# A gated SSM-convolution and token-mixing kernel on one Trainium2 core: more sums by accumulating transfers, small vector work on ScalarE, another fixed order

## The chip, the cores and the metric

The kernel runs on one core of a Trainium2 chip (trn2). The metric is the device time of one execution in microseconds (us); the kernel before took 177.37 us, the median of three runs (177.35 to 178.18). Profiles are of one execution each. The engines are called as the profile calls them: PE (TensorE, with its weight loads as PEld), DVE (VectorE), ACT (ScalarE), POOL (GpSimd) and SP (SyncE, which here only issues transfers).

## What is computed

Two branches over S = 2048 tokens and D = 640 channels are mixed by a gate:

```python
x = A_q                                              # (1, 2048, 640) bf16, like k and v
g = sigmoid((x * gate_w).sum(-1, keepdims=True))
# branch a: k is shifted by a 4-tap causal filter, multiplied with v, then convolved over the
# tokens with a kernel of length 2048 per channel (reference: FFTs of length 4096)
kv = k_shift * v
a  = q * (irfft(rfft(kv) * rfft(ssm_k)) + kv * ssm_D)
# branch b: layer norm of x over channels, then an MLP over the tokens (2048 -> 1536 -> 2048)
h = layernorm(x)
u = gelu(einsum("bsd,sf->bdf", h, w1) + b1)
b = (einsum("bdf,fs->bds", u, w2) + b2).transpose
out = g * a + (1 - g) * b
```

## The kernel before

**Tiling.** A token row tile is 128 tokens by 640 channels; there are 16, in four groups hk of four (p = 0 to 3), all in SBUF in `X`. The matrix `ssm` (640 channels by 2048 taps) is loaded in five blocks of 128 channels, which I number 0 to 4. The transforms are matrix products with cosine and sine tables: `FE` is made on the chip, `FO` is loaded (two transfers of 256 KB), `GTB` holds the inverse tables.

**Stages on PE.** (1) A few matmuls on zeros (`spin`), then per ssm block two transpositions (`transp`, eight 128x128 matmuls for each half h of the taps) and four table products (`wblock`, 16 matmuls each); ACT or DVE copies every result out of PSUM: `wT` after a transposition, `Wb` after a table product. For h = 0, POOL first adds `ssm_D` to column 0 of the block, and that value comes from a tiny matmul and the ACT copy `dcol`. (2) The first MLP product (`m1`: 12 tiles of F, four groups of eight 128x320 matmuls each; ACT applies gelu and writes `GT`), mixed with the shift filter (`kv`, which needs the DMA transposes of k in `KT`) and the forward transforms (`A`). (3) The second MLP product (`m2`, 16 tiles of 24 matmuls; ACT writes `O1` with scale `omg` and bias `c2`). (4) The inverse transforms (`inv`), for h = 0 and h = 1 and four values of p; ACT scales each by the gate (`cg`), DVE multiplies by q and the sum with `O1` leaves by a transfer of 320 KB.

**DVE** does the layer-norm statistics (`ln_tile`: two bn_stats of 320 columns and a bn_aggr per tile), part of the normalization (`ln_apply`), the sums and differences of the transforms (`mixing`, `invmix`, `halved`), the complex products (`product`, `cross`) and the end of the last tile (`last_stt`). A tensor_tensor works on 2560 or 5120 columns there. Some sums are not done on DVE but by a transfer that POOL issues and that adds into its destination (`accum=True`): `v1mix`, `mixing_acc`, `acc_dma`, the second half of some products (the `late` branch), and the output of h = 0.

**What sets the order.** Everything is first recorded as operations with numbers, then emitted in the order of the string `_ORDER` (line 1318 on); each engine runs its own instructions in that order and waits by semaphores for what it depends on. `_ENG` says for 50 operations (copies from PSUM, normalizations, permutations of k) whether ACT or DVE does them, `_SLOTS` which of four PSUM buffers each group of matmuls takes; the group must wait until that buffer's last contents are copied out. So one late operation holds back everything behind it on its engine. SP issues the loads in the same order, and the loads of the start all go through one queue.

**Lines in the profile.** L298 is every matmul, L556 every tensor_tensor, L600 ACT's `act`, L615 and L616 the copies of `either` on ACT and DVE, L627 `last_stt`, L267 an accumulating transfer, L272 a plain one, L265 a DMA transpose, L897 and L899 the statistics, L914 and L915 the normalization on ACT and DVE.

**The last tile.** Row tile (hk 3, p 2) is multiplied last, as two times twelve matmuls: one half of the 640 columns, then the other (`last_`), each 320 wide. `last_stt` combines each half with scale and gate part, and one transfer writes the 160 KB.

Of the kernel before, what the change touches and what calls it, by code (L numbers as in the profile page):

```python
# [9 lines left out]
BF16 = mybir.dt.bfloat16  # L10
# [422 lines left out]
def _build(nc, A_q, A_k, A_v, A_shift_k, A_ssm_k, A_ssm_D, B_x, B_w1, B_b1, B_w2, B_b2, gate_w, out):  # L433
# [10 lines left out]
    with ExitStack() as es:  # L444
# [27 lines left out]
        def base_of(h):  # L472
            return T.mem[h.name][1]
# [24 lines left out]
        cst = alloc("cst", [128, 2], F32)  # L498
# [27 lines left out]
        ksh = [alloc(f"ksh{i}", [128, 4, D], BF16, at=base_of(GT) + 5120 * (1 + i)) for i in range(2)]  # L526
        rows = alloc("rows", [20, 5, 512], BF16, at=base_of(GT))
# [139 lines left out]
        def dr(t, off, ap):  # L667
            return bass.AP(tensor=t.tensor, offset=t.offset + off, ap=ap)
# [23 lines left out]

        def x_load(hk):
            dma(X[:, hk, :, :], qrow(hk), 128 * 5120, chain=True, rate=(352.0 if hk == 0 else 415.0))
# [28 lines left out]
        ssm_load(0, 0, 1)  # L723
        for a, b in ((0, 1), (1, 4)):
            dma(X[:, 0, a:b, :], dr(A_q, a * D, [[4 * D, 128], [1, (b - a) * D]]), 128 * 1280 * (b - a), chain=True)
        ssm_load(1, 0, 1)
        for db in range(1, ND):
            dma(ssm[:, db, :], dr(A_ssm_k, 128 * S * db, [[S, 128], [1, S]]), 128 * 4096, chain=True)
        for p in range(2):
            dma(FO[:, p, :, :, :, :].rearrange("q a b c d -> q (a b c d)"), dr(odd_tab, 1024 * p, [[2048, 128], [1, 1024]]), 128 * 2048, chain=True)  # L730
        for hk in range(1, 4):
            x_load(hk)
# [14 lines left out]
        memset("DVE", cst[:, 1:2], -0.5)  # L747
        iota = lambda ap, pat, b, cm: nolock("POOL", 0.1 + n_of(ap) / 1100.0, lambda s: T.op("POOL", lambda e: e.iota(ap, pat, base=b, channel_multiplier=cm), [], [ap]), [], [ap])
# [152 lines left out]

        def ln_scale(a, b):
            n = b - a
            ts("POOL", sd[:, a:b], mv[:, a:b, 1], 1e-5, None, ALU.add, prio=0)
            o_ = tt("POOL", rstd[:, a:b], sd[:, a:b], V(cst, 1, [[0, n]]), ALU.pow, prio=0)
            o_.dur, o_.lock = 1.75, False
            tt("POOL", sd[:, a:b], sd[:, a:b], rstd[:, a:b], ALU.mult, prio=SDP)
            tt("POOL", nb[:, a:b], mv[:, a:b, 0], rstd[:, a:b], ALU.mult)
            ts("POOL", nb[:, a:b], nb[:, a:b], -1.0, None, ALU.mult)
# [17 lines left out]
        for h in range(2):  # L927
# [5 lines left out]
            if h == 0:  # L933
# [20 lines left out]
                def stats_of(k):  # L954
                    for t in range(LB[k], LB[k + 1]):
                        b0, b1, ag = ln_tile(t // 4, t % 4)
                        b0.after.update(seq[-1:])
                        seq.append(b0)
                        flush()
                        b1.after.update(seq[-1:])  # L960
                        seq.append(b1)
                        pag.append(ag)
                    ln_scale(LB[k], LB[k + 1])
# [12 lines left out]
                mixing(C[0], SS, 0, fine=True, prio=MIXP)  # L976
# [104 lines left out]
        ts("DVE", gpre[:, :], mv[:, :, 0], gws[:, 0:1], None, ALU.mult, mode=1)  # L1081
        tt("DVE", gpre[:, :], gpre[:, :], gth[:, :], ALU.add, mode=1, prio=0)
        act(gth[:, :], gpre[:, :], ACT.Tanh, scale=0.5, prio=0)
        ts("DVE", gg[:, :], gth[:, :], 0.5, 0.5, ALU.mult, ALU.add, mode=1, prio=0)
        ts("DVE", omg[:, :], gth[:, :], -0.5, 0.5, ALU.mult, ALU.add, mode=1, prio=0)
# [20 lines left out]

        INVP = ((0, 2, 1, 3), (1, 3, 0, 2))
        for hk, p in [(hk, p) for hk in range(2) for p in range(4)] + [(hk, p) for p in INVP[1] for hk in (2, 3)]:
# [7 lines left out]
            for a in range(na):  # L1116
                items = []
                for ft, ci in order[a * (24 // na):(a + 1) * (24 // na)]:
                    items.append((chk(ci), w2t(hk, p, ft), GT[:, ft, 320 * ci:320 * ci + 320], ft == 0, ft == FT - 1))
                mms(vt, items, name="m2")  # L1120
                if last_:
                    vt.keep = True
                    lastvt.append(vt)
# [22 lines left out]
        def product(dst, a, v, late=None, into=None):  # L1146
# [14 lines left out]
            tt("DVE", P2(T1), P2(a), P2(v, True), ALU.mult)  # L1161
            tt("DVE", H(dst, 0), H(T0, 0), H(T0, 1), ALU.subtract)
            tt("DVE", H(dst, 1), H(T1, 0), H(T1, 1), ALU.add)
# [32 lines left out]
        def invmix(Ya, Yb, sc, bfirst=False, behind=None):  # L1196
# [8 lines left out]
            for (hy, sy), k in (((hb, sb), 1), ((ha, sa), 0)) if bfirst else (((ha, sa), 0), ((hb, sb), 1)):  # L1205
                tt("DVE", sl(hs, ss + k), sl(hy, sy), sl(hy, sy + 1), ALU.add)
                tt("DVE", sl(hy, sy), sl(hy, sy), sl(hy, sy + 1), ALU.subtract)
# [27 lines left out]
        def inverse(h, Z, G=None):  # L1235
            for p in INVP[h]:
# [24 lines left out]
                tt("DVE", qv if h == 0 else cg[:, :, :], cg[:, :, :], qv, ALU.mult)  # L1261
                if h == 1 and p == INVP[1][-1]:
# [4 lines left out]
                    for ci in range(2):  # L1267
                        last_stt(O1[:, 3, p, 320 * ci:320 * ci + 320], chk(ci), omg[:, t:t + 1], cg[:, 1, 320 * ci:320 * ci + 320], lastvt[ci])
                    dma(rows_of(1, p, 1, 1), O1[:, 3, p, :], 128 * 1280, sem="out")
                elif h == 0:  # L1270
                    dma(ov, qv, 128 * 2560, stream="POOL", prio=0, accum=True)
                    dma(rows_of(0, p, 0, 2), ov, 256 * 1280, sem="out")
# [19 lines left out]
        chained(product, A1[1], A1[1], V0[1], tmp_of(q_hi, 0), V1[1])  # L1292
        chained(product, A1[0], A1[0], V0[0], tmp_of(q_hi, 1), V1[0])
        acc_dma(A1[1], V1[1])
        acc_dma(A1[0], V1[0])
        chained(product, A0[1], A0[1], V0[1], H(V0[1], 0))
        lastacc = SC.ops[-1]
        assert lastacc.eng == "POOL"
        for kt in range(2):
            dma(q_hi[:, kt, :, :], qrow(kt), 128 * 5120, wait=[H(A0[1], 1)]).deps.add(lastacc)  # L1300
        chained(product, A0[0], A0[0], V0[0])
        for kt in range(2):
            dma(q_lo[:, kt, :, :], qrow(2 + kt), 128 * 5120)
# [37 lines left out]
"""  # L1341
_ENG = "DAAAAADDAAAAAADDDDDAAADDDADDDDADDAAAAAAAAAAAAAAADD"
_SLOTS = "1120021323201331122022011133001030332021001010110220110131230121002123231321103301332230032032101133201012203121332133113300113"
# [26 lines left out]
```

## Time and profile before

| | |
|---|---|
| median of the runs (lowest to highest) | 177.37 us (177.35 to 178.18) |
| the profiled execution | 177.12 us |
| its span in the profile | 175.1 us |
| PE / PEld busy | 170.0 / 138.2 us |
| DVE / ACT / POOL busy | 168.9 / 107.6 / 42.7 us |
| granted PE clock | full in all 40 slices |
| moved by transfers | 44.06 MB, mean 252 GB/s |
| accumulating transfers, 640 KB | 15: 8 C<-C, 4 C<-q_hi, 3 C<-SS; median 8.8, 9.7 and 7.4 us from issue to landing |
| accumulating transfers into O, 320 KB | 4; median 4.3 us |

The profiled execution took 2.0 us more than its span; that part lies around the span. Times below are from the span's start. "Busy" counts the instructions' own times: matmuls are pipelined, so a busy PE may still be held up between two of them, and the distance between the starts of two groups is the better measure of PE's pace.

### The profile page before, as it was taken

Reading aid. Unit: us, or ns where it says so; the run is one execution under the profiler, and the core shown is the slowest. Engines: PE = TensorE matmul, PEld = TensorE weight load, DVE = VectorE, ACT = ScalarE, POOL = GpSimd, SP = SyncE. Lnnn points to the kernel's source line nnn. Section 1 sums busy time; section 2 is a strip of 40 time slices with the busy share of each in tenths; the row PEclk is TensorE's granted clock in tenths of the full one; section 3 lists DMA queues with packets and bytes.
Section 4 is the critical chain, followed back from the end, with each engine's and each line's share of the span. In section 5 each row is a group of like instructions: output and inputs, shape, how many; then the busy total and the mean of one; then the engine's idle time right before and its main releaser. Section 6 shows DMA issues by size and latency. Waiting matters only on the chain.

```text
span 175.1 us, 3683 instructions
## 1 busy us (share of the span) xinstructions
PE 170.0 (97%) x1559; PEld 138.2 (79%) x1559; DVE 168.9 (96%) x187; ACT 107.6 (61%) x160; POOL 42.7 (24%) x62
## 2 busy tenths in 40 slices
PE   7999999999899999999999999999999999999992
PEld 2599999877697767777777778888899998698782
DVE  7899999999999999999999999999999999999984
ACT  4499999997999997877556214222215105645760
POOL 3199891000000650003202202220055000052200
PEclk9999999999999999999999999999999999999999
DMA  5999999999999799992999999999939999549598
GB/s 144 397 421 405 376 200 225 380 375 221 179 383 356 172 192 192 186 358 57 178 174 365 353 211 349 282 207 240 300 108 187 197 177 372 241 65 209 106 233 292
DMA packets 33248, 44.06 MB, mean 252 GB/s; under 512 B 12112, under 2 KB 24656, under 8 KB 33104
## 3 DMA queue, kind: packets, MB, share of 16 engines
q1 hardware_dynamic: 28024, 32.68, 57.6%
q0 software_dynamic: 5168, 11.14, 37.4%
q8 instruction: 12, 0.20, 0.4%
q14 instruction: 4, 0.03, 0.1%
q10 hardware_dynamic: 40, 0.01, 0.0%
HBM read 27.44 MB, written 2.62 MB: 172 GB/s over the span
## 4 chain that ended last, share of the span: by engine, by line
PE 93%; DMA 3%; ACT 2%; DVE 0%; DVEq 0%; SPq 0%; issue 0%
PE pp L298 93%; DMA ssm<-in_A_ssm_k_dram 3%; ACT L600 1%; ACT ksh L600 1%; ACT GT L600 0%; DVE O L627 0%; DVEq L426 0%; SPq L272 0%
## 5 line engine op out<-in xcount | busy, mean ns | idle before, releaser
L298 PE MATMUL pp<-X,ring 128*128 128x320 bf16 x384 | 55.4, 299 | 0.5 <-ACT GT L600 0.5
L556 DVE TENSOR_TENSOR C<-C 128x2560 bf16<-128x2560 bf16 (+2 forms) x38 | 54.6, 1485 | 0.3 <-ACT C L600 0.2
L298 PE MATMUL pp<-GT,W 128*128 128x320 bf16 x384 | 53.6, 299 | 0.0
L298 PEld LDWEIGHTS pp<-GT,W 128*128 128x128 bf16 x384 | 48.0, 129 | 4.6
L298 PEld LDWEIGHTS pp<-X,ring 128*128 128x128 bf16 x384 | 37.0, 98 | 15.0 <-ACT GT L600 0.8
L600 ACT ACTIVATE O<-pp,c,omg 128x640 bf16<-128x640 f32 x15 | 12.9, 883 | 24.8 <-PE pp L298 24.8
L267 POOL DMA_DIRECT2D C<-C x8 | 10.5, 1674 | 51.1 <-DVE C L556 30.0
L600 ACT ACTIVATE C<-pp 128x640 bf16<-128x640 f32 x32 | 20.4, 711 | 2.0 <-PE pp L298 2.0
L600 ACT ACTIVATE cgb<-pp,gg 128x640 bf16<-128x640 f32 x16 | 12.1, 795 | 13.3 <-PE pp L298 7.6
L615 ACT ACTIVATE C<-pp 128x1024 bf16<-128x1024 f32 x18 | 17.1, 1051 | 0.3 <-PE pp L298 0.3
L600 ACT ACTIVATE gq<-gq 128x640 bf16<-128x640 bf16 x16 | 11.6, 727 | 5.7 <-DVE gq L556 5.7
L556 DVE TENSOR_TENSOR tm<-C,C 128x5120 bf16<-128x5120 bf16 x5 | 14.1, 2819 | 0.1
L897 DVE BATCH_NORM_STATS2 stats<-X 128x6 f32<-128x320 bf16 x32 | 13.1, 470 | 0.4 <-DMA X<-in_A_q_dram 0.2
L298 PE MATMUL pp<-wT,FO 128*128 128x128 bf16 x160 | 12.4, 219 | 0.0
L600 ACT ACTIVATE GT<-pp,cc 128x640 bf16<-128x640 f32 x12 | 9.3, 793 | 4.8 <-PE pp L298 4.7
L298 PE MATMUL pp<-C,GTB 128*128 128x320 bf16 x80 | 11.9, 299 | 0.0
L298 PE MATMUL pp<-wT,FE 128*128 128x128 bf16 x120 | 11.7, 219 | 0.0
L556 DVE TENSOR_TENSOR SS<-C 128x2560 bf16<-128x2560 bf16 x8 | 11.7, 1482 | 0.0
L267 POOL DMA_DIRECT2D O<-q_hi x4 | 4.8, 1324 | 27.7 <-DVE q_hi L556 27.7
L600 ACT ACTIVATE ksh<-pp 128x1024 bf16<-128x1024 f32 (+1 forms) x12 | 10.1, 908 | 1.4 <-PE pp L298 1.3
L267 POOL DMA_DIRECT2D C<-q_hi x4 | 4.8, 1198 | 23.8 <-DVE q_hi L556 10.9
L556 DVE TENSOR_TENSOR C<-tm 128x2560 bf16<-128x2560 bf16 x7 | 10.3, 1487 | 0.1
(92 smaller groups left out, 225.3 us busy)
## 6 DMA issues: line engine op xcount, KB each, us to landing
ring<-in_B_w_dram SPq DMA_DIRECT2D x12, 512.0 KB, 8.8
W<-in_B_w_dram SPq DMA_DIRECT2D x12, 512.0 KB, 6.8
C<-C POOLq DMA_DIRECT2D x8, 640.0 KB, 8.8
kn<-in_A_k_dram SPq DMA_DIRECT2D x4, 640.0 KB, 9.6
C<-q_hi POOLq DMA_DIRECT2D x4, 640.0 KB, 9.7
out_dram<-O SPq DMA_DIRECT2D x7, 320.0 KB, 3.2
ssm<-in_A_ssm_k_dram SPq DMA_DIRECT2D x4, 512.0 KB, 7.0
X<-in_A_q_dram SPq DMA_DIRECT2D x3, 640.0 KB, 7.3
```

The lines of the kernel that those rows point to most:

```text
L267: ins = engobj.dma_start(out_ap, in_ap, accum_op=ALU.add, max_dma_last_dim=2560)
L298: ins = self.nc.tensor.matmul(ps_ap, lhsT=lhsT, rhs=rhs, start=start, stop=stop, skip_group_check=True)
L556: o_ = SC.add(eng, d, lambda s: T.op(eng, lambda e: e.tensor_tensor(o, a, b, op), rd, [o]), rd, [o], prio=prio, name="tt")
L600: return T.op("ACT", lambda e: e.activation(o, src, func, **kw), rr + [src], ww)
L615: return either(name, o, i, [], lambda e, src: e.activation(o, src, ACT.Copy, **kw), lambda e, src: e.tensor_copy(o, src) if scale == 1.0 ...
L897: ops.append(SC.add("DVE", 0.38, (lambda o, i: lambda s: T.op("DVE", lambda e: e.bn_stats(o, i), [i], [o]))(o, i), [i], [o]))
```

## The change

- **Loads.** X group 1 in place of group 0 is loaded in two pieces, ssm block 4 in place of block 0 in two halves (`xpart`, `ssm_load`).
- **Row tile 11** (hk 2, p 3) has its mean and variance made on ACT (`ln_tile_act`, three instructions) instead of on DVE (three).
- **Gate.** `gpre`, `gg` and `omg` are scaled on ACT instead of DVE; a constant 0.5 is set by POOL.
- **Mixing** of `C[0]`: one sum and one difference of 5120 columns instead of two of 2560 each; the same in `invmix` for the second half.
- **Products.** All four now take the branch with an accumulating transfer; A0[0] took the one without. A0 comes first, then A1 with its sum by transfer; the q loads follow.
- **Output of h = 1.** For p = 1 and 3 the sum with `O1` is an accumulating transfer and then the output transfer, in place of a DVE sum.
- **Last tile.** 512 and 128 columns in place of 320 and 320, and two output transfers.
- **Order.** New `_ORDER`, `_ENG` and `_SLOTS`. In the new order the operation `table`, a tiny gelu that makes ACT load that function's table, stands right behind the sine that makes `FE`; in the old one it stood behind the first gelu results. SP's first loads are: before X group 2, ssm block 1, half of block 0, block 2, the two FO, X group 3, block 3, X group 1, 480 KB of X group 0; after X group 2, ssm block 0, half of block 4, X group 0, block 3, 160 KB of X group 1, the two FO, 480 KB of X group 1, block 1, X group 3, block 2.

```diff
-        ssm_load(0, 0, 1)
+        ssm_load(0, 4, 5)
         for a, b in ((0, 1), (1, 4)):
-            dma(X[:, 0, a:b, :], dr(A_q, a * D, [[4 * D, 128], [1, (b - a) * D]]), 128 * 1280 * (b - a), chain=True)
-        ssm_load(1, 0, 1)
-        for db in range(1, ND):
+            dma(X[:, 1, a:b, :], xpart(1, a, b), 128 * 1280 * (b - a), chain=True)
+        ssm_load(1, 4, 5)
+        for db in [d for d in range(ND) if d != 4]:
...
+        def ln_tile_act(t):
+            xs = X[:, t // 4, t % 4, :]
+            r = 1.0 / math.sqrt(D)
+            act(junk[:, :], xs, ACT.Copy, scale=1.0 / D, acc=mv[:, t, 0:1], name="lnm")
+            act(cst[:, 2:3], mv[:, t, 0:1], ACT.Copy, scale=-r, name="lnb")
+            act(junk[:, :], xs, ACT.Square, scale=r, bias=cst[:, 2:3], acc=mv[:, t, 1:2], name="lnm")
...
-                mixing(C[0], SS, 0, fine=True, prio=MIXP)
+                mixing(C[0], SS, 0, prio=MIXP)
...
-        ts("DVE", gpre[:, :], mv[:, :, 0], gws[:, 0:1], None, ALU.mult, mode=1)
+        act(gpre[:, :], mv[:, :, 0], ACT.Copy, scale=gws[:, 0:1])
         tt("DVE", gpre[:, :], gpre[:, :], gth[:, :], ALU.add, mode=1, prio=0)
         act(gth[:, :], gpre[:, :], ACT.Tanh, scale=0.5, prio=0)
-        ts("DVE", gg[:, :], gth[:, :], 0.5, 0.5, ALU.mult, ALU.add, mode=1, prio=0)
-        ts("DVE", omg[:, :], gth[:, :], -0.5, 0.5, ALU.mult, ALU.add, mode=1, prio=0)
+        act(omg[:, :], gth[:, :], ACT.Identity, scale=-0.5, bias=cst[:, NCST:NCST + 1], prio=0)
+        act(gg[:, :], gth[:, :], ACT.Identity, scale=0.5, bias=cst[:, NCST:NCST + 1], prio=0)
...
+        LASTC = (0, 512, 640)
...
+                    c0, c1 = LASTC[ci:ci + 2] if last_ else (320 * ci, 320 * ci + 320)
...
+            if ha is hb and sb + 2 == sa:
+                y0, y1 = (V(ha, (sb + j) * SL, [[2 * SL, 2], [1, SL]]) for j in range(2))
+                tt("DVE", V(hs, (ss + 1) * SL, [[-SL, 2], [1, SL]]), y0, y1, ALU.add)
+                tt("DVE", y0, y0, y1, ALU.subtract)
...
-                tt("DVE", qv if h == 0 else cg[:, :, :], cg[:, :, :], qv, ALU.mult)
+                by_dma = h == 0 or p in (1, 3)
+                tt("DVE", qv if by_dma else cg[:, :, :], cg[:, :, :], qv, ALU.mult)
...
-                        last_stt(O1[:, 3, p, 320 * ci:320 * ci + 320], chk(ci), omg[:, t:t + 1], cg[:, 1, 320 * ci:320 * ci + 320], lastvt[ci])
-                    dma(rows_of(1, p, 1, 1), O1[:, 3, p, :], 128 * 1280, sem="out")
-                elif h == 0:
+                        c0, c1 = LASTC[ci:ci + 2]
+                        last_stt(O1[:, 3, p, c0:c1], (lambda s, ci=ci, n=c1 - c0: s[:, 512 * ci:512 * ci + n]), omg[:, t:t + 1], cg[:, 1, c0:c1], lastvt[ci])
+                        o_ = rows_of(1, p, 1, 1)
+                        dma(bass.AP(tensor=o_.tensor, offset=o_.offset + c0, ap=[list(o_.ap[0]), [1, c1 - c0]]), O1[:, 3, p, c0:c1], 128 * 2 * (c1 - c0), sem="out")
+                elif by_dma:
                     dma(ov, qv, 128 * 2560, stream="POOL", prio=0, accum=True)
-                    dma(rows_of(0, p, 0, 2), ov, 256 * 1280, sem="out")
+                    dma(rows_of(h, p, 0, 2), ov, 256 * 1280, sem="out")
...
-        chained(product, A1[1], A1[1], V0[1], tmp_of(q_hi, 0), V1[1])
-        chained(product, A1[0], A1[0], V0[0], tmp_of(q_hi, 1), V1[0])
-        acc_dma(A1[1], V1[1])
-        acc_dma(A1[0], V1[0])
-        chained(product, A0[1], A0[1], V0[1], H(V0[1], 0))
...
-        chained(product, A0[0], A0[0], V0[0])
...
+        for g in range(2):
+            chained(product, A0[g], A0[g], V0[g], tmp_of(tm[1], g))
+        for g in (1, 0):
+            chained(product, A1[g], A1[g], V0[g], tmp_of(q_hi, g), V1[g])
+            acc_dma(A1[g], V1[g])
```

More of the change, by code (lines that the diff above doesn't have):

```diff
@@ L497, in _build @@
         c2 = alloc("c2", [128, 16], F32)
-        cst = alloc("cst", [128, 2], F32)
+        NCST = 3
+        cst = alloc("cst", [128, NCST + 1], F32)
         FE = alloc("FE", [128, 2, 2, 2, 128], BF16)
@@ L526, in _build @@
         ksh = [alloc(f"ksh{i}", [128, 4, D], BF16, at=base_of(GT) + 5120 * (1 + i)) for i in range(2)]
+        junk = alloc("junk", [128, D], BF16, at=base_of(GT) + 10240)
         rows = alloc("rows", [20, 5, 512], BF16, at=base_of(GT))
@@ L691, in qrow, with xpart @@
             return row8(A_q, hk) if hk >= 2 else dr(A_q, 512 * hk * D, [[4 * D, 128], [1, 4 * D]])
+        def xpart(hk, a, b):
+            t = qrow(hk)
+            return bass.AP(tensor=t.tensor, offset=t.offset + a * D, ap=[list(t.ap[0]), [1, (b - a) * D]])
         def x_load(hk):
@@ L730, in _build @@
             dma(FO[:, p, :, :, :, :].rearrange("q a b c d -> q (a b c d)"), dr(odd_tab, 1024 * p, [[2048, 128], [1, 1024]]), 128 * 2048, chain=True)
-        for hk in range(1, 4):
+        for hk in [k for k in range(4) if k != 1]:
             x_load(hk)
@@ L747, in _build @@
         memset("DVE", cst[:, 1:2], -0.5)
+        memset("POOL", cst[:, NCST:NCST + 1], 0.5)
         iota = lambda ap, pat, b, cm: nolock("POOL", 0.1 + n_of(ap) / 1100.0, lambda s: T.op("POOL", lambda e: e.iota(ap, pat, base=b, channel_multiplier=cm), [], [ap]), [], [ap])
@@ L900, in ln_tile @@
             return ops
+        ACT_TILE = 11
+        def ln_tile_act(t):
[4 more added lines that the diff above has]
+            act(junk[:, :], xs, ACT.Square, scale=r, bias=cst[:, 2:3], acc=mv[:, t, 1:2], name="lnm")
         def ln_scale(a, b):
@@ L955, in stats_of @@
                     for t in range(LB[k], LB[k + 1]):
+                        if t == ACT_TILE:
+                            ln_tile_act(t)
+                            continue
                         b0, b1, ag = ln_tile(t // 4, t % 4)
@@ L1118, in _build @@
                 for ft, ci in order[a * (24 // na):(a + 1) * (24 // na)]:
-                    items.append((chk(ci), w2t(hk, p, ft), GT[:, ft, 320 * ci:320 * ci + 320], ft == 0, ft == FT - 1))
+                    c0, c1 = LASTC[ci:ci + 2] if last_ else (320 * ci, 320 * ci + 320)
+                    items.append(((lambda s, ci=ci, n=c1 - c0: s[:, 512 * ci:512 * ci + n]), w2t(hk, p, ft), GT[:, ft, c0:c1], ft == 0, ft == FT - 1))
                 mms(vt, items, name="m2")
@@ L1160, in product @@
                 return
-            tt("DVE", P2(T1), P2(a), P2(v, True), ALU.mult)
-            tt("DVE", H(dst, 0), H(T0, 0), H(T0, 1), ALU.subtract)
-            tt("DVE", H(dst, 1), H(T1, 0), H(T1, 1), ALU.add)
         C3a = (C[2], 0)
@@ L1204, in invmix @@
             (ha, sa), (hb, sb), (hs, ss) = Ya, Yb, sc
-            for (hy, sy), k in (((hb, sb), 1), ((ha, sa), 0)) if bfirst else (((ha, sa), 0), ((hb, sb), 1)):
+            if ha is hb and sb + 2 == sa:
+                y0, y1 = (V(ha, (sb + j) * SL, [[2 * SL, 2], [1, SL]]) for j in range(2))
+                tt("DVE", V(hs, (ss + 1) * SL, [[-SL, 2], [1, SL]]), y0, y1, ALU.add)
+                tt("DVE", y0, y0, y1, ALU.subtract)
+            for (hy, sy), k in () if ha is hb and sb + 2 == sa else (((ha, sa), 0), ((hb, sb), 1)):
                 tt("DVE", sl(hs, ss + k), sl(hy, sy), sl(hy, sy + 1), ALU.add)
@@ L1291, in _build @@
         lastp = []
-        chained(product, A1[1], A1[1], V0[1], tmp_of(q_hi, 0), V1[1])
-        chained(product, A1[0], A1[0], V0[0], tmp_of(q_hi, 1), V1[0])
-        acc_dma(A1[1], V1[1])
-        acc_dma(A1[0], V1[0])
-        chained(product, A0[1], A0[1], V0[1], H(V0[1], 0))
[L1297 to L1300, printed above, removed]
-        chained(product, A0[0], A0[0], V0[0])
-        for kt in range(2):
-            dma(q_lo[:, kt, :, :], qrow(2 + kt), 128 * 5120)
+        for g in range(2):
[3 more added lines that the diff above has]
+            acc_dma(A1[g], V1[g])
+        for hk in range(2):
+            dma(q_hi[:, hk, :, :], qrow(hk), 128 * 5120)
+        for hk in range(2):
+            dma(q_lo[:, hk, :, :], qrow(2 + hk), 128 * 5120)
         Z0 = invmix(A0[0], A0[1], C3a)
@@ L1318 @@
 _ORDER = """
[22 rows of a table removed]
-"""
-_ENG = "DAAAAADDAAAAAADDDDDAAADDDADDDDADDAAAAAAAAAAAAAAADD"
-_SLOTS = "1120021323201331122022011133001030332021001010110220110131230121002123231321103301332230032032101133201012203121332133113300113"
[22 rows of a table added]
+"""
+_ENG = "DAAAAAAAAADAAAADDDAADADDDADDDDDDDAAAADAAAAAADAAADD"
+_SLOTS = "1201310233133112220101332302223010103212121222230303212002330011323320230022021133130312011210310231230003021101331133131100331"
 _INS = ['A_q', 'A_k', 'A_v', 'A_shift_k', 'A_ssm_k', 'A_ssm_D', 'B_x', 'B_w1', 'B_b1', 'B_w2', 'B_b2', 'gate_w']
```

44 rows, old and new, of the table _ORDER are left out of this document.

## The prediction

> **What bounds the kernel.** I read the page first (busy shares, slices, chain), then the chain of waits in order of time, then the starts of PE's groups in the timeline, then ACT and the loads of the first 32 us.
>
> ```profile
> span 175.1 us, 3683 instructions
> ...
> PE 170.0 (97%) x1559; PEld 138.2 (79%) x1559; DVE 168.9 (96%) x187; ACT 107.6 (61%) x160; POOL 42.7 (24%) x62
> ...
> PE 93%; DMA 3%; ACT 2%; DVE 0%; DVEq 0%; SPq 0%; issue 0%
> ```
>
> PE and DVE are both nearly full, but the chain runs over PE alone. In order of time it shows where PE is not the one:
>
> ```profile
> 1.19 5.37 DMA ssm<-in_A_ssm_k_dram
> ...
> 42.13 1.28 ACT L600
> 43.41 0.01 issue
> 43.43 0.81 ACT GT L600
> 44.23 0.05 issue
> 44.28 127.63 PE pp L298 x988
> 171.91 0.02 issue
> 171.93 0.55 DVE O L627
> ```
>
> PE waits for the first ssm block until 6.6, pauses at 44 for ACT (a table load, then a gelu that frees a PSUM buffer), and ends at 171.9; then come two DVE instructions and one transfer. Between 6.6 and 171.9 the starts of PE's groups keep one pace: 0.50 us for a transposition, 0.89 for a table product, 1.09 for eight 128x320 matmuls. The only larger hole is the one at 44: groups start at 42.38 and 44.27, 1.89 apart, so 0.8 is lost. So less work on DVE or ACT gains nothing by itself; the change can gain that 0.8, some tenths elsewhere, or the tail, and it loses what it makes PE wait. I therefore add up PE's lag against the kernel before.
>
> **The front: loads and first copies.** Landing is the issue time plus the time to landing in the transfer view, one transfer at a time:
>
> ```profile
> X<-in_A_q_dram SPq DMA_DIRECT2D x1, 640.0 KB, 8.8
> X<-in_A_q_dram SPq DMA_DIRECT2D x1, 480.0 KB, 10.7
> ssm<-in_A_ssm_k_dram SPq DMA_DIRECT2D x1, 512.0 KB, 12.5
> ```
>
> Issued at 5.51, 5.99 and 7.01 they landed at 14.3, 16.6 and 19.5. One after the other, the loads give 1.60 us for 640 KB, 1.30 for 512, 0.66 for 256, 0.44 for 160; the piece of 480 KB took 2.34, twice its share, and all behind it stayed late. The three that come first (640, 512, 256 KB, landed 5.30, 6.55, 7.21) have the same sizes after the change. Then the new order gives: X group 0 at 8.8, block 3 at 10.1, 160 KB of X at 10.55, FO at 11.2 and 11.86, the 480 KB at 14.2, block 1 at 15.5, X group 3 at 17.1, block 2 at 18.4.
>
> (a) First transposition: before, it needed only the landed block (6.60). Now block 0 comes first and POOL's add stands ahead (row 6.63, 0.20): 6.87. Its copy is DVE's (1.19), after the matmuls' end at 7.6: 8.85. The first table product starts at 8.9 with three transpositions done; before, at 9.54 with five. 8.9 - 9.54 + 2 x 0.50 = **+0.36**.
>
> (b) From 8.9, two products and two transpositions bring PE to 11.68, where the first product with FO stands: FO lands at 11.86, **+0.25**. Before, FO was there at 9.8, ahead of its use.
>
> (c) Then three products (2.67), and at 14.6 PE stands before a transposition of block 1, which lands at 15.5: **+0.85**. If the 480 KB took their share (1.2), block 1 would land at 14.35 and this is 0. I take 0.85: it is a load of the same shape.
>
> (d) ACT cannot make up for it. It is as full as PE here:
>
> ```profile
> 7.36 2.99 ACT L615 ACTIVATE wT<-pp 128x1024 bf16<-128x1024 f32 x3 [1.08 <-PE pp L298]
> ...
> 29.13 2.89 ACT L615 ACTIVATE C<-pp 128x1024 bf16<-128x1024 f32 x3
> 31.84 0.97 ACT L914 ACTIVATE X<-X,nb,rstd 128x640 bf16<-128x640 bf16 x1
> ```
>
> 26 copies go from 7.36 to 32.0, 0.905 apart when in a row, and the first m1 starts at 30.2, its four tiles normalized by DVE. In the new order one of these tiles is ACT's, behind 24 copies. After block 1, PE has 15 products, 5 transpositions and 0.11 before m1: 15.5 + 16.0 = 31.5. ACT has 16 copies from 16.25 on: 30.7 without a wait, 31.2 with those that PE's alternation makes; then the normalization (0.97): 31.7 to 32.2. **+0.65** (from 0, if ACT never waits and normalizes while PE finishes, to 1.0, the whole instruction).
>
> Sum of the front: +2.1.
>
> **ACT's table and row tile 11.** The second table load now follows the sine: sine ends at 4.73, load 1.28, the tiny gelu, `dcol` at 6.2 in place of 5.93; POOL's add waits for the block until 6.55 anyway, so 0.3 of cover is left. The pause at 44 goes: **-0.8**; next late there is ACT's copy queue, 14.5 of 15 us busy in the 45-to-60 window, so nothing more. The Trainium skill (ScalarE: Activation LUTs, What ACT_TABLE_LOAD costs) puts a switch at about 2.66 us, the load and a drain. This trace has no drain: the copy ahead ends at 42.11, the load runs 42.13 to 43.41, gelu starts at 43.43. By the page, as an estimate, `dcol` would come at 7.6 and the front would lose about 1.0 more; by the row it loses nothing, and the row decides (rival 5). Statistics of tile 11 on ACT: 0.72 (row gq, with its sum), 0.22 (tanh row), 0.73 to 0.98 (rows gq and X): ACT is free again at about 8.1, and its first copy waits for PE until 8.25. Cost 0, or 0.3 without that cover. DVE is relieved of two statistics at 0.40 and 0.10.
>
> **The rest of DVE.** The gate moves 0.57 (rows 0.23, 0.17, 0.17) to ACT, which waits for PE 24.8 us in its o1 group alone; but `c2` now stands behind a q_hi product on DVE, at about 115.6, where the first o1 waits for it: 0 to 0.5, I take 0, since PE reaches it later too. Merging four 2560s into two 5120s (1.40 apart against 2.74) saves 0.1 per pair. A0[0] by transfer saves one 5120 less one 2560: 1.37. Two output sums go: 1.64. In all DVE loses 4.6 us of work, none of it on the path, so worth 0 by itself. The price is on the other side: the new order puts the first inverse group that needs the last sum of `invmix` after 140.4 us of PE work, against 146.9 before. DVE has 3.0 us less to do until that sum, which ended at 147.2: 144.2, and about 1.3 more for waits that it inherits from the loads (X group 3 at 17.1) and from late ACT copies: 145.5. PE, 1.3 late, is there at 140.4 + 4.05 + 1.3 = 145.7 (4.05: start less work done, in the last groups before). A tie, and the same again at the last inverse groups: **+0.3**, from 0 to 3. Below 0 it cannot be, a wait ends no earlier than PE.
>
> **Accumulating transfers.** POOL's issue takes 1.20 each and POOL is free. A0[1]'s lands 6.2 to 10.8 after its issue (the rows of 640 KB); DVE wants it some 7 after: 0 to 3, part of the range above. The new output sums land 4.3 after, with 320 KB to go out (2.6 to 3.8): about 176 in the span at worst, level with the end.
>
> **The tail.** Two combinations of 320 took 1.01 together (0.55 each). In the new order DVE's 128 columns come first, then the 512, both behind the last matmul; with the same slope 0.27 + 0.75 = 1.02. The last transfer is 1024 instead of 1280 bytes per row: 0. Had the 512 come first, 0.6 would be gained; the order does not do so.
>
> **Sum.** +0.36 + 0.25 + 0.85 + 0.65 - 0.8 + 0.3 = +1.6 on the profiled execution's 177.12 us: **178.7 us**. The median of the runs, 177.37, is 0.25 above that execution.
>
> **Rivals.** (1) The front holds: the 480 KB land in their turn, and ACT's normalization is hidden by PE's last products. Then +0.36 - 0.8: 176.7, faster than before. It decides if block 1 lands before 14.6 and the tile is normalized before 31. For it: the bytes alone would allow it, 400 GB/s in these slices. Against it: the measured 2.34, and ACT's full row. 0.12. (2) The 480 KB land in their turn, the rest as forecast: 177.12 + 0.75 = 177.9. 0.20. (3) DVE or a transfer sets the end: a sum of A0 waits for its transfer, late by up to 3, and every inverse group with it: about 180.5. For it: the tie above and 44 MB in transfers; against it: the last C<-SS sum before, a transfer of the same kind, was issued at 128.9 and landed at 135.0, and its reader on DVE started only at 138.6. 0.13. (4) The last tile does what its cut suggests, a tail shorter by 0.6: the order speaks against it, 0.03. (5) ACT stands as long before the early table load as the load takes (1.28): `dcol` at 7.5, and the first transposition 0.9 later still: 179.6. Against it: 0.02 between the copy and the load at 42; 0.02. The page's drain is this case.
>
> **Chances and range.** Forecast 0.50. A measurement of this kernel can tell about 0.5% (0.9 us) from no change: 176.5 to 178.3. Faster: 0.07 (rival 1 with some tenths more, and rival 4); within: 0.33 (rivals 1 and 2, the low end of the forecast); slower: 0.60. The range 176.9 to 180.2 leaves out the far ends of rivals 1 and 3.
>
> **What would show it.** Right: PE's wait for ssm at about 14.6 (or for FO at 11.7), first m1 at about 32, no table load at 42 and no gap at 44, last matmul near 173.2, 1.0 us of DVE behind it. Wrong: block 1 landed by 14.4, m1 at 30.5, or PE waiting for DVE around 145 and 162 for more than 1 us.

## The result, and the profile after

The changed kernel took **179.27 us** (median of 6 runs, 178.69 to 179.83), the kernel before 177.36 beside it: ratio 1.0105, 95% interval 1.0075 to 1.0135. The forecast was 178.7, range 176.9 to 180.2. The profiled execution took 178.69 with a span of 176.9, 1.8 more than before; it is the quickest of the six, so the median lies 0.6 above it. From the page after (span, busy shares, shares of the chain that ended last):

```profile
span 176.9 us, 3687 instructions
...
PE 170.6 (96%) x1559; PEld 137.4 (78%) x1559; DVE 165.1 (93%) x176; ACT 110.2 (62%) x167; POOL 50.1 (28%) x66
...
DVE 51%; PE 21%; DMA 12%; issue 7%; SPq 3%; POOL 2%; ACT 2%; DVEq 0%
```

DVE has 3.8 us less work (the forecast had 4.6), and yet the chain now runs over DVE for half of the span, where PE alone had 93%. That share does not make DVE's work the limit: the chain comes to DVE only through the issue of the transfer that lands at 150, and this transfer stood in a queue (e5). The chain after, in order of time (start, length, what):

```profile
6.12 12.13 DMA ssm<-in_A_ssm_k_dram
...
18.31 0.20 POOL ssm L558
18.51 1.01 POOL rstd L558
...
20.06 1.32 POOL rstd L558
...
21.71 0.17 POOL ssm L558
...
139.49 0.73 POOL C L267
140.22 9.88 DMA C<-C
...
150.22 2.83 DVE SS L558
...
159.48 2.90 DVE SS L558 x2
...
162.43 10.84 PE pp L298 x78
...
173.30 0.35 DVE O L629
```

Three things stand there that the chain before did not have: a load that lands at 18.25, with POOL's queue behind it until 21.88; a transfer that DVE waits for until 150.1; and PE waiting for DVE until 162.4. PE's own waits in the changed kernel (us in total, times, longest):

```profile
PE pp L298 <- DMA ssm<-in_A_ssm_k_dram: 0.6, 1, 0.6
PE pp L298 <- DVE SS L558: 0.6, 1, 0.6
PE pp L298 <- POOL ssm L558: 0.2, 1, 0.2
```

To place the loss I use the forecast's own measure, PE's **lag**: the start of a group of matmuls less the work of all groups ahead of it at their usual pace. A step of lag is about 0.16 longer than the idle time in the list above, because a matmul's record lasts that much longer than the distance to the next one (0.299 against 0.136 for 320 columns). Only steps and differences count here: the level drifts a little where a group's usual pace is set too high or too low, in both kernels alike.

| place | before | after | difference |
|---|---|---|---|
| first table product (9.5 / 8.5 us) | 3.62 | 3.56 | -0.06 |
| first transposition of block 1 | | 3.86 | |
| of block 2 | | 4.70 | |
| behind POOL's sum at 21.9 | | 5.09 | |
| start of m1 | 3.68 | 5.12 | +1.44 |
| ahead of 44 us | 3.49 | 4.74 | +1.25 |
| behind 44 us | 4.29 | 4.86 | +0.57 |
| inverse groups at 147 | 4.04 | 4.55 | +0.51 |
| inverse groups at 163 | 4.04 | 5.36 | +1.32 |
| end of PE | 171.89 | 173.27 | +1.38 |
| end of the span | 175.1 | 176.9 | +1.8 |

So 0.5 is left of the front once the pause at 44 is gone, 0.8 comes at 163 and 0.4 behind the last matmul. The pause itself was 0.67, not the 0.8 of the table's column and of the prediction: in the kernel before, the groups around it start at 42.52 and 44.28, 1.76 apart with 1.09 of work (the prediction read 42.38 and 44.27).

### The profile page after: what moved, and what is told of

Read it like the earlier page. It is cut to its first block, busy times and chain, and to the rows that moved or that the text cites. A ratio compares the mean times of both kernels' runs of the same rounds, so it can differ in the third digit from the quotient of the medians.

```text
span 176.9 us, 3687 instructions
## 1 busy us (share of the span) xinstructions
PE 170.6 (96%) x1559; PEld 137.4 (78%) x1559; DVE 165.1 (93%) x176; ACT 110.2 (62%) x167; POOL 50.1 (28%) x66
## 4 chain that ended last, share of the span: by engine, by line
DVE 51%; PE 21%; DMA 12%; issue 7%; SPq 3%; POOL 2%; ACT 2%; DVEq 0%
DVE C L558 30%; PE pp L298 21%; DVE tm L558 11%; DMA ssm<-in_A_ssm_k_dram 7%; DMA C<-C 6%; DVE SS L558 3%; DVE q_hi L558 3%; SPq L272 3%; DVE gq L558 3%; ACT C L602 2%; POOL rstd L558 1%; DVE kv L558 1%; POOL C L267 0%; DVEq L426 0%; POOL ssm L558 0%
## 5 line engine op out<-in xcount | busy, mean ns | idle before, releaser
L298 PE MATMUL pp<-GT,W 128*128 128x320 bf16 (+2 forms) x384 | 53.5, 299 | 0.0
L298 PEld LDWEIGHTS pp<-GT,W 128*128 128x128 bf16 x384 | 47.3, 129 | 5.4
L617 ACT ACTIVATE C<-pp 128x1024 bf16<-128x1024 f32 x17 | 16.5, 1052 | 0.0
L904 DVE BATCH_NORM_STATS2 stats<-X 128x6 f32<-128x320 bf16 x30 | 12.4, 473 | 1.2 <-DMA X<-in_A_q_dram 1.2
L298 PE MATMUL pp<-wT,FO 128*128 128x128 bf16 x160 | 12.9, 219 | 0.0
L558 DVE TENSOR_TENSOR tm<-C,C 128x5120 bf16<-128x5120 bf16 (+1 forms) x5 | 12.8, 2551 | 0.0
L558 DVE TENSOR_TENSOR SS<-C 128x2560 bf16<-128x2560 bf16 (+1 forms) x6 | 11.4, 1933 | 1.2 <-DMA C<-C 1.1
L298 PEld LDWEIGHTS pp<-C,GTB 128*128 128x128 bf16 x80 | 7.7, 98 | 3.1 <-DVE C L558 0.2
L298 PEld LDWEIGHTS pp<-wT,FO 128*128 128x128 bf16 x160 | 10.0, 98 | 0.1
```

The costliest lines, as they stand in the source:

```text
L298: ins = self.nc.tensor.matmul(ps_ap, lhsT=lhsT, rhs=rhs, start=start, stop=stop, skip_group_check=True)
L558: o_ = SC.add(eng, d, lambda s: T.op(eng, lambda e: e.tensor_tensor(o, a, b, op), rd, [o]), rd, [o], prio=prio, name="tt")
L617: return either(name, o, i, [], lambda e, src: e.activation(o, src, ACT.Copy, **kw), lambda e, src: e.tensor_copy(o, src) if scale == 1.0 ...
L904: ops.append(SC.add("DVE", 0.38, (lambda o, i: lambda s: T.op("DVE", lambda e: e.bn_stats(o, i), [i], [o]))(o, i), [i], [o]))
```

## The experiments

All times are medians, set against the kernel before on the same chip (176.94 to 177.02); the changed kernel was not run again there, and 1.0105 of that is 178.8 to 178.9. The expectations of e1 to e4 were counted from 177.36 and 179.27, the medians above, so there the gain is to be compared and not the time. Numbers in the order are operations.

### e1: block 2 ahead of X group 3

```diff
-... 40 14 49 8 140 ...
+... 40 8 14 49 140 ...
```

> The changed kernel with one load moved: ssm block 2 is issued ahead of X group 3. Theory (PE waits for a late ssm block in the front, and POOL, which waits for the same block, then keeps back the sum of block 1 by its statistics work): block 2 lands at 16.9 in place of 18.24, PE's lag behind its own work when m1 begins falls from 5.1 to 3.9 us, and the time falls by 0.8 to 1.2: 178.1 to 178.5. Rival (DVE's statistics are as near to the bound: X group 3 lands 1.3 later and DVE already waits 1.2 for it): m1 or the chain on DVE becomes late by the same amount, 179.0 to 179.5. Second question, which load the 16 KB transfer of the queue named instruction holds back: the one in flight at 14.1 to 15.7, whatever it carries.

**Measured:** 180.04 us, ratio 1.017 (1.0148 to 1.0192): 1.2 slower than the changed kernel, worse than either expectation. Block 2 landed at 16.76, and PE's lag before its transposition was down to 3.92; then PE lost 2.0 at one stroke. The waits of PE, and DVE's instructions at that time, both of e1:

```profile
PE pp L298 <- DVE C L618: 1.8, 1, 1.8
```

```profile
18.35 0.49 DVE L904 BATCH_NORM_STATS2 stats<-X 128x6 f32<-128x320 bf16 x1 [2.71 <-DMA X<-in_A_q_dram]
18.76 1.21 DVE L618 TENSOR_SCALAR C<-pp 128x1024 bf16<-128x1024 f32 x1
```

**What follows:** the theory falls. The rival's cause, the late X group 3, is the one, by another path and at a higher price. DVE waits 2.71 for X group 3 with a statistic, and behind it in DVE's queue stands a copy of a table product (L618), for whose PSUM buffer PE waits. In the changed kernel the same copy ended at 18.6, just as block 2 had come: two waits of the same length, one behind the other.

### e2: last tile in two PSUM buffers, 512 columns first

```diff
             for a in range(na):
+                if last_ and a:
+                    vt = _VT("mlp")
-... 530 643 642 617 646 644 647 645
+... 530 643 642 617 644 645 646 647
```

The second buffer also takes one more entry in `_SLOTS`.

> The changed kernel with the two parts of the last tile in two PSUM buffers, and DVE's 512 columns and their transfer ahead of the 128. By the prediction's words 0.6 would be gained. Theory now: DVE is busy with the row tile before until 173.1 and can start the 512 columns only 0.2 ahead of PE's end, so DVE ends at 174.1 in place of 174.3, and the last transfer is 32 KB in place of 128: 0.2 to 0.5 gained, 178.8 to 179.1.

**Measured:** 178.83 us, ratio 1.0124 (1.0097 to 1.0151), level with the changed kernel: none of the expected gain of 0.2 to 0.5. That 178.83 lies in the expected range is chance, since the range was counted from 179.27. The 512 columns started at 173.30, at PE's end (173.35), since DVE was busy until 173.18, and DVE ended at 174.31 (174.30 in the changed kernel). **What follows:** the order of the two parts was not what the tail hung on, and in this order the 0.6 of the prediction was not there to be had.

### e3: the last C<-C sum on DVE

```diff
-                dma(o, i_, 128 * 5120, stream="POOL", prio=0, accum=True)
+                if i and hd is C[3] and sd == 2:
+                    tt("DVE", o, o, i_, ALU.add)
+                else:
+                    dma(o, i_, 128 * 5120, stream="POOL", prio=0, accum=True)
-... 564 505 573 ... 588 ...
+... 505 573 ... 588 564 ...
```

> The changed kernel with the last of the eight C<-C sums on DVE, behind the first q_hi product of the output, where DVE waits for that transfer. Theory (the first SS<-C of the second invmix waits until 150.1 for the transfer, and by it PE loses 0.75 before the inverse groups of h = 1): it starts at about 149, PE's step of lag at 163 goes, 0.6 to 0.8 gained: 178.5 to 178.7. Rival (that DVE chain is late anyway, by work and waits for ACT's scaled copies): the sum's 1.4 us on DVE take the place of the wait, 179.2 to 179.6.

**Measured:** 178.26 us, ratio 1.0074 (1.0053 to 1.0094), its span 0.9 below the changed kernel's. DVE's instructions around 150, first in the changed kernel, then in e3 (the bracket is DVE's idle time before the instruction, and what ended it):

```profile
148.28 0.83 DVE L558 TENSOR_TENSOR q_hi<-cgb,q_hi 128x1280 bf16<-128x1280 bf16 x1 [1.40 <-ACT cgb L602]
150.22 2.83 DVE L558 TENSOR_TENSOR SS<-C 128x5120 bf16<-128x5120 bf16 x1 [1.11 <-DMA C<-C]
```

```profile
145.62 1.48 DVE L558 TENSOR_TENSOR C<-C,C 128x2560 bf16<-128x2560 bf16 x1
...
148.21 0.82 DVE L558 TENSOR_TENSOR q_hi<-cgb,q_hi 128x1280 bf16<-128x1280 bf16 x1 [0.37 <-ACT cgb L602]
148.95 2.82 DVE L558 TENSOR_TENSOR SS<-C 128x5120 bf16<-128x5120 bf16 x1
```

The same sum of the second `invmix` in the kernel before, with no idle time ahead of it:

```profile
147.13 2.89 DVE L556 TENSOR_TENSOR SS<-C 128x2560 bf16<-128x2560 bf16 x2
```

**What follows:** the theory. The sum costs DVE 1.48 at 145.62, where it idled for ACT anyway, the wait for the transfer is gone, and the step of lag at 163 with it: PE ends at 172.39 in place of 173.27. By the medians alone the gain, about 0.5, would not be clear, as the two intervals overlap; the traces show it, and so does the pair e6 and e7 below.

### e4: the kernel before with the early table

```diff
-... 42 36 59 ... 340 38 341 ...
+... 42 36 38 59 ... 340 341 ...
```

> The kernel before with one instruction moved: the tiny gelu stands behind the sine, as in the changed kernel. Theory (the pause of PE at 44 is the table load, and a load at the start is hidden): PE's lag stays at 3.5 past 44 and the time falls by 0.8: 176.5 to 176.7. Rival (what PE gains at 44 is lost again, to ACT's copies or to DVE further on): 177.2 to 177.4. Rival (a switch at the start costs a drain too): 177.4 or more.

**Measured:** 176.81 us, ratio 0.9988 (0.9966 to 1.0009), single runs from 176.04 to 177.73. In its profile the pause at 44 is gone, and 0.6 of it comes back at 49. PE's groups in e4:

```profile
42.48 2.34 PE L298 MATMUL pp<-X,ring 128*128 128x320 bf16 x16
...
49.24 1.45 PE L298 MATMUL pp<-KF,KT 128*128 128x128 bf16 x26 [0.62 <-DMA KT<-kp]
```

The last transpose of k was issued at 42.6 in both kernels and took 4.94 before and 6.56 here. **What follows:** the first rival. The pause covered another wait close behind it. The rival's range was counted from the higher median; beside 176.94 it means no gain, and 0.1 was measured, which the interval does not tell from none. The quickest run lies 0.9 below the median of the kernel before and 0.5 below its quickest (176.50), as if it had no such wait; only one run was profiled, and it has it.

### e5: POOL's sum of block 1 first

```diff
-... 217 75 149 ... 187 68 69 ...
+... 217 68 75 149 ... 187 69 ...
```

> The changed kernel with POOL's sum of ssm block 1 (needed by one transposition) ahead of its sum of block 2, instead of behind block 2 and two rstd operations. Theory (POOL's queue costs PE 0.4 at 21.9: the sum ends at 21.87, and PE had come at 21.5): that step of lag goes, the time falls by 0.4, 178.4 where the changed kernel stands at 178.8 beside this chip's 176.9. Rival (ACT's row of copies and the normalization it ends with, until 32.0, set the first m1 anyway): 0 to 0.1.

**Measured:** 178.99 us, ratio 1.0096 (1.0069 to 1.0123). The step at 21.9 goes: the lag behind it is 4.68 in place of 5.09, and 4.30 at 148 in place of 4.55. At 163 it is 5.40, as in the changed kernel (5.36). **What follows:** in time the rival, for another reason than it gave. POOL's queue did cost 0.4 in the front, and m1 starts 0.25 earlier (31.44 in place of 31.69). The time does not show it, because the transfer sets what comes after: POOL issued the last sum at 139.97 in place of 140.22, and it landed at 150.15 in place of 150.10, in both 9.5 behind the first of the four sums that stand in the queue there. DVE's SS<-C started at 150.27, in the changed kernel at 150.22.

### e6 and e7: the front mended, without and with e3

e6 is e1 and e5 and one move more; e7 is e6 with e3's edit.

```diff
-... 216 123 161 199 219 206 ...
+... 216 123 199 219 161 206 ...
```

> The changed kernel with three moves: ssm block 2 ahead of X group 3 (as in e1), DVE's copy of a table product ahead of the statistics that wait for X group 3, and POOL's sum of block 1 ahead of block 2's. Theory (in e1 PE waited 2.0 for that copy, which stood behind the statistics): the 2.0 go, and with the two other steps PE's lag at the first m1 falls from 5.1 to 4.0 by the loads alone, or to about 4.5 by ACT, which has only 0.6 of idle time between 8 and 32; time 178.8 less 0.6 to 1.1, 177.7 to 178.2. Rival (the late X group 3 still holds DVE, or DVE's chain up to 139 sets the end whatever PE does in the front): 178.6 to 179.2.

> e6 and e3 together: the front's three moves, and the last C<-C sum on DVE. If the lag of the front and the wait for the transfer at 150 are separate costs, their gains add up: about 1.2 to 1.6 below the changed kernel, 177.2 to 177.6, level with the kernel before within 0.4%. Rival (the one hides the other, since DVE and the transfers run on their own): no better than the better of e3 and e6.

**Measured:** e6 179.16 us, ratio 1.0123 (1.009 to 1.0157), no better than the changed kernel; e7 177.90, ratio 1.0035 (1.0019 to 1.0051). In e6's profile PE's lag is 4.22 behind POOL's sum and 4.78 at m1, so the loads and POOL were mended, and 0.6 comes back between, the largest step (0.4) at a copy on DVE that PE waits for. At 148 it is 4.22 and at 163 5.08: the step is there again. In e7 it is 4.39 and 4.40.

**What follows:** the one edit of e3 takes 1.26 us from e6, with intervals far apart, so the wait for the transfer is a cost of its own, and with this front the larger part of the loss. It is more than the step of 0.86 in e6's profile. That profile is of the quickest of six runs (178.38, the median is 0.78 above it), so the wait may be longer in the others; no trace of a slower one was kept, and this is not shown. The spread of the runs does not settle it: e7 lies within 0.44 and e6 within 1.59, but e5, which has the transfer, lies within 0.45.

Of e7's two expectations the rival falls, since e7 is below e3. It stands 1.0 below the changed kernel by the medians and 1.2 by the ratios, at or just under the low end of the theory's 1.2 to 1.6. Still the gains are not two numbers that simply add: the front's three moves gain nothing while the transfer is in the way (e6), and behind e3 they gain 0.4 by the medians and 0.7 by the ratios (1.0074 and 1.0035); the spans of the two profiles differ by 0.1 only. What is left of e7's loss stands in its profile as 0.4 at PE's end (172.31 against 171.89) and 0.4 behind it, and no run here removes it.

### e8: e4 with a group of m1 ahead of the kv groups

```diff
-... 276 284 316 ... 369 ...
+... 276 284 369 316 ...
```

> e4 (the kernel before with the early table) with one group of m1 matmuls of PE ahead of the kv groups that wait for the transposes of k. Theory (in e4 what was gained at 44 was lost in part at 49, where PE waited for the transposes until 49.2): the group of 1.09 fills that wait, and the full 0.8 is kept: 176.1 to 176.3 beside 176.9. Rival (the loss is further on, on ACT or DVE): as e4, 176.8.

**Measured:** 177.48 us, ratio 1.0022 (1.0001 to 1.0043). The wait for the transposes is gone, the lag 3.24 at 53; between 53 and 58 it rises to 4.35, with PE waiting for ACT's copies (ksh). **What follows:** the rival's cause, at a higher price than it had, 0.46 above the kernel before. Behind the pause at 44 lie the transposes of k, and behind these ACT's copies: in this order the gain at 44 does not pass them.

### e9: a group of m2 ahead of the inverse groups

```diff
-... 511 625 618 512 ... 615 519 630 616 628 638 520 636 ...
+... 511 625 519 618 512 520 ... 615 630 616 628 638 636 ...
```

> The changed kernel with one m2 group (and the copy of its tile on ACT) moved ahead of the inverse group at 162 that waits for the sum on DVE. Theory (PE stands 0.75 to 1 us there, in some executions more, for the transfer that landed at 150.1): 1.09 us of work lie in the wait, PE's step of lag at 163 goes as in e3, and ACT's last copies come 0.9 earlier: 0.8 to 1.3 below the changed kernel (178.8 on such a chip), 177.6 to 178.0. Rival (whatever comes late on DVE there is late for all that follows, so moving work only moves the wait): 178.6 or more.

**Measured:** 179.26 us, ratio 1.0127 (1.0105 to 1.015): nothing gained. PE in e9, behind the place where the wait was:

```profile
162.54 4.51 PE L298 MATMUL pp<-SS,GTB 128*128 128x320 bf16 x32
166.89 1.84 PE L298 MATMUL pp<-C,GTB 128*128 128x320 bf16 x12
169.02 0.72 PE L298 MATMUL pp<-C,GTB 128*128 128x320 bf16 x4 [0.29 <-ACT cgb L602]
```

**What follows:** the rival. The lag is 4.7 until 168, so the wait for DVE was filled; but the moved group had stood between short inverse groups and given ACT the time to copy their buffers out. Without it PE waits for ACT (lag 5.27, then 5.42), and its end stays at 173.25.

### e10: e7 with e9's move and e2's tail

The three diffs are those of e7, e9 and e2 together.

> e7 with the moved m2 group of e9 and the tail of e2 (two PSUM buffers, 512 columns first). Theory: in e2 nothing was gained because DVE was busy until 173.1 with a row tile that waited for ACT's last copies; with the m2 copy out of ACT's way DVE is free 0.7 before PE ends, so the 512 columns lie beside PE's last matmuls and the end comes 0.5 earlier than in e7 (177.9): 177.3 to 177.5. Rival (the outputs' issue on SP sets the end): 177.8 to 178.0.

**Measured:** 179.13 us, ratio 1.0116 (1.0097 to 1.0135), worse than e7 by 1.2. PE's end moves from 172.31 to 173.17, by the same two waits for ACT as in e9 (0.6) and a front 0.15 later in this execution. The tail itself worked: DVE ended 0.78 behind PE in place of 1.03, but SP's issues stood one behind the other from 171.30 to 175.29 without a gap, and the last transfer was issued at 174.64 (DVE had ended at 173.95). **What follows:** the first half falls as e9 did, and the rival of the second half, SP's issues, holds.

### e11: e7 with the late table

```diff
-... 55 7 39 41 ... 243 375 237 ...
+... 55 7 41 ... 243 375 39 237 ...
```

> e7 with the tiny gelu behind the first gelu results, so that the table is loaded at 44 as in the kernel before. If the prediction's term holds in the changed kernel (0.8 lost at 44 and kept): 178.7 beside e7's 177.9. If the pause is absorbed further on, as in e4 and e8 (ACT's copies and the transposes of k come next): 178.0 to 178.2.

**Measured:** 178.31 us, ratio 1.0079 (1.0054 to 1.0105). In the profile the load costs PE nothing; ACT in e11:

```profile
42.64 1.02 ACT L602 ACTIVATE ksh<-pp 128x1024 bf16<-128x1024 f32 x1 [0.36 <-PE pp L298]
43.68 1.28 ACT L602 ACT_TABLE_LOAD   x1
44.98 1.48 ACT L602 ACTIVATE GT<-pp,cc 128x640 bf16<-128x640 f32 x2
```

In e7 the same gelu started at 44.34, so ACT had had 0.6 to spare; PE's groups kept their pace, lag 5.03 ahead of it and 5.04 behind. The profiled execution lies 0.46 above e7 already at 43, because its first ssm block landed at 6.75 in place of 6.12. **What follows:** in the profiled execution the place of the table makes no pause in the new order. The median lies 0.1 above the second expectation and far below the first; whether the 0.4 over e7 has a part from the table stays open.

### e12: e4 with the tail in two parts

The tail is e2's (512 first, two PSUM buffers, two transfers), built into e4.

```diff
+        LASTC = (0, 512, 640)
+                if last_ and a:
+                    vt = _VT("mlp")
-... 647 646 648
+... 646 647 648 649
```

> The kernel before with the early table of e4 and its last tile as 512 and 128 columns in two PSUM buffers, 512 first, two transfers. In the kernel before DVE is free at 171.7, 0.2 ahead of PE's end. Theory: DVE ends 0.2 earlier and the last transfer is 32 KB; with e4's 0.1 to 0.4, 176.4 to 176.7 beside 177.0, the best of all. Rival (two issues on SP and transfers of 256-byte rows cost what is won): 176.8 to 177.0.

**Measured:** 177.07 us, ratio 1.0003 (0.9985 to 1.0021), runs from 176.18 to 177.79. **What follows:** no gain that shows; in its profile PE waits 0.6 for w1 and 0.7 for the transposes. That profile is of the slowest of its runs. No kernel here is clearly faster than the one before; e4, whose interval reaches across 1, comes nearest.

## Why the forecast came out, step by step

The time was inside the range and 0.6 above the forecast. That the sum came so near is in part luck. Three of its terms, (a), (b) and (d), +1.26 together, came to nothing; POOL, block 2, the transfer and the tail, which it did not have or had smaller, filled the gap. The outer signs came as named (m1 at 31.7, last matmul at 173.3, DVE 1.03 behind it), and they do not tell the two apart. The wait at 162 is the mechanism of rival 3, to which the prediction gave 0.13, at 0.8 in the profile in place of up to 3.

- **(a) and (b), +0.36 and +0.25: nothing, and less than 0.1.** Block 0 landed at 6.05, 0.5 ahead of the row that I had taken from the profile before; later traces of this load order have it from 5.99 to 7.06, and PE's lag at m1 was about the same at both ends (5.04 in e3 with 7.06, 5.12 in the changed kernel). The second half of FO landed at 11.73, and PE stood 0.07 for it at 11.78.
- **(c), +0.85: +0.28 at block 1 and +0.84 at block 2.** The mechanism was PE waiting for ssm blocks, and that is what it did, but with the wrong reason for the loads: the 480 KB took 1.21, their share, as in rivals 1 and 2, and X group 3, behind block 1, took 2.72. Block 1 landed at 14.21, and PE waited for it all the same, as it was there at about 14.0 in place of the forecast's 14.6. What makes such a transfer late is not its shape (last section).
- **Not foreseen: POOL, +0.39.** Block 2's sum stands in POOL's order ahead of five more operations and then block 1's sum. A wait that is added to a queue has to be followed through it; I did that for ACT and DVE, not here. e5 shows it.
- **(d), +0.65: nothing.** ACT's normalization ended at 32.00, inside the forecast's 31.7 to 32.2; but PE, with 0.39 more of its own delay, came at 31.7, and needed that tile last in its group. e6 shows that the copies out of PSUM stand right behind: of 0.9 won in the loads and at POOL, 0.3 was left at m1.
- **(e), -0.8: -0.7, and for another reason.** The pause was 0.67, a misreading of 0.1. It is gone, but the profile of e11 has the load at 44 and no pause: in the new order ACT idles there. In the old order, where the forecast looked, the early table is worth 0.1, not clear of none (e4), since the transposes of k come next, then ACT's copies. The line that put ACT's copy queue next, "so nothing more", left the transposes out. The step on the start was right: sine to 4.74, load 4.76 to 6.04, `dcol` at 6.16 (forecast 6.2), with no drain on either side; rival 5 falls. The Trainium skill (ScalarE: Activation LUTs, What ACT_TABLE_LOAD costs) gives about 2.66 us for a switch, a drain included; this trace does not agree, its switch took the 1.28 of the load.
- **(f), +0.3: nothing at 145, 0.8 and more at 163.** The last sum of the first `invmix` ended at 145.04 (forecast 145.5), the tie held. At the last inverse groups it did not. The failed step is the one that put the accumulating transfers at "0 to 3, part of the range above": it weighed A0's transfer and not A1's. Before, one of A1's four sums of 640 KB had landed at 124.35 and the last at 145.95, 1.2 ahead of the DVE sum that reads it (147.13). Now all four are issued from 130.77 on, beside loads that are in flight until 138.84; they land one behind the other at 140.6, 143.8, 146.9 and 150.1, and all of the second `invmix`, for which DVE was free at 149.1, stands behind them. e3 shows it, and e7 beside e6 with a price of 1.26.
- **The tail, 0: +0.4.** DVE ended 1.03 behind PE, as before (1.05). But the last issue now waits 0.2 for SP, which issues four output transfers in a row, and its 128 KB took 2.1 to land where 160 KB in one piece had taken 1.8. That 0.6 would have been won with the 512 columns first did not hold in this order (e2).

The sum of the measured steps: +1.44 in the front, -0.68 at 44, -0.25 around it, +0.81 at 163, +0.06 to PE's end, +0.42 behind it: 1.8, the difference of the spans. Most of the -0.25 is a wait of 0.17 that PE had at 33.8 in the kernel before, for a copy of the shift filter on ACT, and has no longer.

## What to carry to other kernels

Work taken from an engine that is not on the chain was worth nothing here, and as it went to accumulating transfers it put the transfers on the chain: look which transfers come last ahead of a wait, and leave a reader time. Here 1.2 us of slack became a wait of 1.1. Where a wait is added, follow the whole queue behind it on its engine (POOL's small sums, DVE's one PSUM copy), because PE meets it there. A pause that is removed is only worth the distance to the next wait, so look at what was finished just ahead of the pause's end. Where the terms of a sum have different signs, check each term and not the total.

## What was not expected of the hardware

**Loads land late beside instruction transfers.** The page after lists a queue named instruction beside the loads' queue (packets, MB, share of 16 engines):

```profile
q8 instruction: 12, 0.20, 0.4%
```

That is 16 KB each, and one occupies its DMA engine for 0.9 to 1.5 us; in the changed kernel the first began at 14.66, in the window of X group 3:

```profile
q8 instruction: 1, 0.02, 2.7%
```

2.7% of 16 engines over 2.4 us is 1.0 us of one engine. In 12 of the 14 traces the load in flight then, or the next, landed 0.8 to 1.5 later than its share, whatever it was: 480 KB of X in the kernel before, X group 3 after, block 2 in e1, e2 and e7, X group 3 again in e6. In e3 and e11, whose loads had been late from the start, it was 0.3 and 0.5. In e4, e8 and e12 a packet at 47.0 to 47.8 lies in the last transpose of k, which took 6.6; in the kernel before it came at 49.7, behind the transpose, which took 4.9. The Trainium skill (Runtime: NRT & Kernel Launch, Instruction fetch mechanics) says that an engine's instruction memory is refilled in 16 KiB blocks and that the cost is mostly hidden. The size agrees, and no wait in the views is put down to this queue; the loads and transposes beside it are late. Which engine the packets are for, no view says. No run here moves such a packet by itself, so that it is the cause is read from times that fall together and is not shown.

**Accumulating transfers ran at half the pace of loads.** Queued one behind the other, the four sums of 640 KB landed 3.16 apart, where a load of 640 KB took 1.60. From 133 to 152 the accumulating transfers kept the transfer engines full in the changed kernel (packets, MB, share of 16 engines):

```profile
q0 software_dynamic: 1583, 3.23, 95.4%
```
